# Computing the first batch's attention output already transposed: denominators from products with ones

## The chip, the cores and the metric

The kernel runs on one core of one Trainium2 chip. The metric is device time in microseconds (us), the median of three runs of the whole program. Before the change it is 306.56 us (306.39 to 308.27).

The engines are named as the profile names them: PE is the matrix engine and PEld its weight loads, DVE the vector engine, ACT the scalar engine, POOL the GpSimd engine (here it copies a little and issues most of the transfers that convert float32 to bfloat16), SP the engine that issues the other transfers.

## The reference, cut to what matters

A sparse attention over 8 batches, 8 heads, 576 positions and 64 dimensions per head is followed by a two-layer MLP over all 4608 tokens.

```python
scores = scale * np.matmul(q, k.transpose(0, 1, 3, 2))
rel = pos[:, None] - pos[None, :]
mask_local   = (rel >= 0) & (rel < 32)                         # heads 0 to 3
mask_strided = (rel >= 0) & (pos[None, :] % 32 == pos[:, None] % 32)   # heads 4 to 7
attn = softmax(where(mask, scores, -1e9))
x = (attn @ v).transpose(0, 2, 1, 3).reshape(B * S, H * D)     # 4608 x 512
h = x @ w_in                                                   # 512 -> 2048
out = (h * np.tanh(softplus(h))) @ w_out                       # 2048 -> 512
```

The MLP needs x with its 512 features on the partitions, which the kernel calls xT: four groups of 128 features (cc 0 and 1 from the local heads, cc 2 and 3 from the strided heads) by the tokens.

## The kernel before

The tokens pass through the MLP in nine blocks of 512. While block t passes, the attention of batch t+1 is done in between. Only the attention of batch 0 has nothing to hide behind: until its xT is there, the MLP cannot start. That opening, and block 0 with the attention of batch 1, are what the change touches.

In the opening, the mask is first put into PSUM by a product with the identity ("bias"), the score products are added to it, and ACT takes exp. The probabilities P then serve as the stationary operand, v (with a 65th column of ones, which gives the denominator) as the moving one. So x comes out with the tokens on the partitions, is divided by the denominator, and is transposed on PE afterwards:

```python
def pv_mm(self, kind, i, po):
    for h in range(4):
        ...
        nc.tensor.matmul(po[:, h, :], lhsT=pt[0:n, c0:c0 + 128], rhs=rhs, start=True, stop=True)

def pv2(self, kind, i, i_acc):
    po = acc(i_acc, "po2")[:, :, 0:4 * (D + 1)].rearrange("p e (h d) -> p e h d", h=4)
    ...
    nc.vector.reciprocal(rden[0:m], po[0:m, :, :, D])            # 8 denominators per partition
    nc.vector.tensor_tensor(out=dst..., in0=po[0:m, :, :, 0:D],
        in1=rden[0:m].unsqueeze(3).to_broadcast([m, 2, 4, D]), op=ALU.mult)

def xt(self, kind, hf, eng=None):
    tr = tile_t("trx")[:].bitcast(BF16)
    ...   # 6 or 8 transposes on PE, then one cast into xT
```

The opening itself, from the score products on (cut):

```python
for i in range(3):
    a.qk([("s", i)], i)               # strided scores and exp
copy_v_str01(0, Dv, 0, 4)             # strided v into its layout of 65 columns, on DVE
copy_v_str01(0, Dv, 4, 8)
fill(tile_t("fill"), 2)               # products of zeros
a.pv2("s", 0, 0)
t_step_loc0(kl0, kTl[:, 0, 32:32 + S], 0, Dv)     # local k transposed
t_step_loc0(kl0, kTl[:, 1, 32:32 + S], 1, Sc)
a.pv2("s", 2, 1)
a.pv2("s", 4, 2)
...
t_step_loc0(ql0, qTl[:, 0, :], 0, Sc)             # local q transposed
t_step_loc0(ql0, qTl[:, 1, :], 1, Sc)
a.pv2("s", 6, 0)
a.bias("l", 0, 1)                     # local masks, scores, exp
...
a.xt("s", 0, Dv)
a.xt("s", 1)
Sc.preload_act_table(AF.Mish)
a.pv2("l", 0, 1)
a.pv2("l", 2, 0)
a.pv2("l", 4, 1)
accs = (2, 0, 1)
gT, g1 = mlp1(0, accs)
g1.pop(0)()                           # first hidden group, cc 2 and 3
a.xt("l", 0)
g1.pop(0)()                           # second hidden group, cc 2 and 3
a.xt("l", 1)
```

There are three large PSUM buffers (acc 0 to 2, two banks each) and two small ones (tile_t, one bank each). They hold the scores, the products with v and, later, the MLP's sums in turn. The MLP's second layer of block 0 goes through w_out in quarters: sixteen products with the first quarter, then sixteen with the second, and so on.

Of the kernel before, what the change touches and what calls it, by code (L numbers as in the profile page):

```python
# [10 lines left out]
F32 = mybir.dt.float32  # L11
BF16 = mybir.dt.bfloat16
# [28 lines left out]
def kernel(ctx, tc, q, k, v, moe_w_in, moe_w_out, out):  # L41
# [35 lines left out]
    P_s = [const.tile([PN, 2, n * PN + 56], BF16, name=f"Ps{i}") for i, n in enumerate((7, 7, 4))]  # L77
    P_l = [const.tile([128, 2, n * WQ + 32], BF16, name=f"Pl{i}") for i, n in enumerate((5, 5, 2))]
    x_l = const.tile([128, NW, 256], BF16, name="x_l")
    x_s = const.tile([128, CS, 256], BF16, name="x_s")  # L80
# [53 lines left out]

    def load_v_loc01(b, w0, w1):
        for w in range(w0, w1):
            nc.gpsimd.dma_start(
                vl[b][32:128, w, :, 0:D], v[b, 0:4, WQ * w:WQ * w + WQ].rearrange("h p d -> p h d")
            )

    def load_v_loc_h(b):
# [4 lines left out]

    def rows_v_loc01(b, w0, w1, eng):
        w0, x = max(w0, 1), vl[b % 2]
        cast(eng, x[0:32, w0:w1, :, 0:D], x[96:128, w0 - 1:w1 - 1, :, 0:D])

# [32 lines left out]
    def cast(eng, out_, in_):  # L183
        if eng is nc.scalar:
            nc.scalar.copy(out_, in_)  # L185
        else:
            eng.tensor_copy(out_, in_)  # L187
# [102 lines left out]
    PARTS["n"] = [S_UNITS[0:7], S_UNITS[7:14], S_UNITS[14:16]]  # L290
    AT = {kd: {u: (i, n) for i, p in enumerate(PARTS[kd]) for n, u in enumerate(p)} for kd in "sln"}

    class Attn:
        def __init__(self, b):
            self.b = b
            self.biased = {}

        def bias(self, kind, i, i_acc):
            ps = self.biased[kind, i] = acc(i_acc, "ps")
            w, n, m = (WQ, 128, loc_b) if kind == "l" else (PN, PN, stm_b)  # L300
            nu = len(PARTS[kind][i])
            for e in range(2):
                nc.tensor.matmul(
                    ps[:, e, 0:nu * w], lhsT=ident[0:n, :],
                    rhs=m.unsqueeze(1).to_broadcast([n, nu, w]), start=True, stop=False,
                )

        def qk(self, parts, i_acc):

            biased = parts[0] in self.biased  # L310

            if i_acc is None:
                ps = [tile_t("ps") for _ in range(2)]
            else:
                t = self.biased[parts[0]] if biased else acc(i_acc, "ps")
                ps = [t[:, 0, :], t[:, 1, :]]
            o, todo = 0, []
            for kind, i in parts:
                w = WQ if kind == "l" else PN
                o0 = o  # L320
                for x, y in PARTS[kind][i]:
                    for e in range(2):
                        r = slice(64 * e, 64 * e + 64)
                        if kind == "l":
                            lhsT, rhs = kTl[r, y, WQ * x:WQ * x + 128], qTl[r, y, WQ * x:WQ * x + WQ]
                        else:
                            c0 = SU * (4 * y + x)
                            lhsT = sT(kTs, self.b + (kind == "n"))[r, c0:c0 + 128]
                            rhs = sT(qTs, self.b + (kind == "n"))[r, c0:c0 + PN]
                        nc.tensor.matmul(  # L330
                            ps[e][:, o:o + w], lhsT=lhsT, rhs=rhs, start=not biased,
                            stop=not biased or (x, y) == PARTS[kind][i][-1],
                        )
                    o += w
                todo.append((kind, i, o0, o - o0))
# [37 lines left out]
        def pv(self, kind, i):  # L373
# [8 lines left out]
                in1=rden[0:m, :].unsqueeze(2).to_broadcast([m, 4, D]), op=ALU.mult,  # L382
            )

        def pv2(self, kind, i, i_acc):

            po = acc(i_acc, "po2")[:, :, 0:4 * (D + 1)].rearrange("p e (h d) -> p e h d", h=4)
            m = WQ if kind == "l" else PN
            for e in range(2):
                self.pv_mm(kind, i + e, po[:, e])  # L390
            dst = (x_l if kind == "l" else x_s)[0:m, i:i + 2, :]
            rden = small.tile([128, 2, 4], F32, tag="rden2", name="rden2")
            nc.vector.reciprocal(rden[0:m], po[0:m, :, :, D])
            nc.vector.tensor_tensor(
                out=dst.rearrange("p e (h d) -> p e h d", h=4), in0=po[0:m, :, :, 0:D],
                in1=rden[0:m].unsqueeze(3).to_broadcast([m, 2, 4, D]), op=ALU.mult,
            )
# [48 lines left out]
        def xt_str_copy(self):  # L446
            t0 = (self.b % RING) * S
            for c in range(2):
                nc.scalar.copy(  # L449
                    xT[:, 2 + c, t0:t0 + S].rearrange("p (n j) -> p j n", j=CS), xs_t[:, :, c, 0:PN]  # L450
                )

    def str_steps(b):

        a = Attn(b)
        V = lambda i: (lambda: a.pv("s", i))
        return [
            [], [V(0)], [V(1)], [V(2)], [V(3)], [V(4)], [V(5)], [V(6)], [V(7), a.xt_str],
        ]
# [22 lines left out]
    def attn_steps(b, x, y, z=None):  # L482
# [6 lines left out]
        s0, s1, sl2, l0, l1 = ("s", 0), ("s", 1), (("s", 2), ("l", 2)), ("l", 0), ("l", 1)  # L489
        if x == y:  # L490
            return [
                [], [Q(x, s0)],
                [M(*s0), Q(x, s1)],
                [V("s", 0)],
                [V("s", 1), M(*s1), Q(x, *sl2)],
                [V("s", 2)],
                [V("s", 3), M("s", 2), M("l", 2), Q(x, l0)],
                [V("s", 4)],
                [V("s", 5), M(*l0), Q(x, l1)],
                [V("s", 6), V("l", 5)],  # L500
                [V("s", 7), V("l", 0), M(*l1)],
                [X("s", 0), V("l", 1)],
                [X("s", 1), V("l", 2)],
                [V("l", 3), V("l", 4)],
                [X("l", 0), X("l", 1)], [],
            ]
        r = [
# [16 lines left out]
        if z is not None:  # L524
            r[12].append(Q(x, ("n", 0)))
            r[13].append(Q(z, ("n", 1)))
            r[15] += [Q(x, ("n", 2)), M("n", 0), M("n", 1), M("n", 2)]
        return r


# [91 lines left out]
    with tc.manual_schedule():  # L622
# [14 lines left out]
        Dv.memset(vl[0][0:32, 0], 0.0)  # L637
        load_v_loc01(0, 0, 3)
        load_w_in(0, 256)
        load_v_loc01(0, 3, 6)  # L640
        load_w_in(256, 512)
        load_w_in(512, 1024)
# [17 lines left out]

        a = Attn(0)
        fill_acc(2, 11)
        for hp in range(2):
            t_step(0, "k", hp, Sc if hp else Dv)
        a.bias("s", 0, 0)
        fill_acc(2, 4)
        for hp in range(2):
            t_step(0, "q", hp, Sc if hp else Dv)
        a.bias("s", 1, 1)
        fill_acc(2, 1)  # L670
        a.bias("s", 2, 2)
        for i in range(3):
            a.qk([("s", i)], i)
        copy_v_str01(0, Dv, 0, 4)
        copy_v_str01(0, Dv, 4, 8)
        fill(tile_t("fill"), 2)
        a.pv2("s", 0, 0)
        t_step_loc0(kl0, kTl[:, 0, 32:32 + S], 0, Dv)
        t_step_loc0(kl0, kTl[:, 1, 32:32 + S], 1, Sc)
        a.pv2("s", 2, 1)  # L680
        a.pv2("s", 4, 2)
        fill_acc(0, 1)
        t_step_loc0(ql0, qTl[:, 0, :], 0, Sc)
        t_step_loc0(ql0, qTl[:, 1, :], 1, Sc)
        a.pv2("s", 6, 0)
        a.bias("l", 0, 1)
        a.bias("l", 1, 2)
        a.qk([("l", 0)], 1)
        a.qk([("l", 1)], 2)
        rows_v_loc01(0, 0, 3, Po)  # L690
        load_w_in(1024, 1536)
        load_w_in(1536, 2048)
        rows_v_loc01(0, 3, 6, Po)
        load_qk_str(1)
        load_w_out(0, 1)
        load_v_str01(1)
        load_qk_loc01(1, rows(kl[1]), rows(ql[1]))
        load_w_out(1, 3)
        load_v_loc_h(1)
        load_w_out(3, 4)  # L700
        a.bias("l", 2, 0)
        a.qk([("l", 2)], 0)
        a.xt("s", 0, Dv)
        a.xt("s", 1)
        Sc.preload_act_table(AF.Mish)
        a.pv2("l", 0, 1)
        a.pv2("l", 2, 0)
        a.pv2("l", 4, 1)
        accs = (2, 0, 1)
        gT, g1 = mlp1(0, accs)  # L710
        g1.pop(0)()
        a.xt("l", 0)
        g1.pop(0)()
        a.xt("l", 1)
        Dv.memset(vl32[0:32], 0.0)
        for x in (ks, qs):
            Dv.memset(x[0][64:SU], 0.0)
        load_qk_str(2)
        rows_v_loc01(1, 0, 6, Po)
        for dst, src in ((kl, k), (ql, q)):  # L720
# [8 lines left out]
        def next_loads():  # L729
            load_qk_str(3)  # L730
            copy_v_str01(2, Po, 0, CS)
            rows_v_loc01(2, 0, 6, Po)

        for t in range(NBLK):
# [4 lines left out]
            if t == 0:  # L739
                ts, at = t_steps1(), attn_steps(1, y, y)  # L740
                at[0] += [lambda: Sc.preload_act_table(AF.Exp)]
                at[1] += [lambda: copy_v_str01(1, nc.vector, 0, CS), next_loads]
                at[2] += ts[4:6]
                at[3] += ts[6:8]
                at[9] += [lambda: str_by_dma(2), lambda: loc_by_dma(2)]
# [77 lines left out]
```

## Time and profile before

| What | Value |
|---|---|
| Time, median of 3 | 306.56 us |
| Span of the profiled run | 306.6 us |
| PE busy | 297.2 us (97%) |
| ACT busy | 182.9 us (60%) |
| DVE busy | 156.8 us (51%) |
| POOL busy | 104.0 us (34%) |
| First product of the MLP | 19.42 us |
| The MLP's first layer runs without a gap from | 22.55 us |
| First product of block 1 | 58.03 us |

The page of the profile gives each engine's busy time, then the chain of work that ended last, then the groups of instructions with the mean duration of one. The timeline of a window lists what each engine did and, in brackets, how long it sat idle before and what ended that. [...] For the opening the timeline matters most, as the shares of the whole span are set by the nine blocks behind it.

### The profile page before, as it was taken

To read this page: it belongs to the slowest core of one execution; us is meant where nothing else is said; L and a number is where in the kernel's file an instruction comes from. 1 tells how busy PE (TensorE), PEld (TensorE's weight loads), DVE (VectorE), ACT (ScalarE), POOL (GpSimd) and SP (SyncE) were. 2 spreads that over 40 slices of the span, in tenths; PEclk is the share of its full clock that TensorE was granted. 3 is DMA by queue.
4 is the path that set the end of the run, shared out by engine and by line. 5 is a ranking of instruction groups with operands and counts; after the bars stand their busy time and mean duration, and the time that the engine had idled before them with its cause. 6 is when DMAs were issued, how large, how long until landed. Compare 5 with 4: busy or idle time off the path is not lost.

```text
span 306.6 us, 5875 instructions
## 1 busy us (share of the span) xinstructions
PE 297.2 (97%) x2431; PEld 154.4 (50%) x2431; DVE 156.8 (51%) x375; ACT 182.9 (60%) x196; POOL 104.0 (34%) x120
## 2 busy tenths in 40 slices
PE   8889999999999999999999999999999999999995
PEld 3544555544554445444578654445444544444444
DVE  3572358201850086579877888787879850000000
ACT  5576553767446763767866786687668746216501
POOL 8592326741246025502980297029600000000000
PEclk9999999999999999999999999999999999999999
DMA  7999999999999999999969996997430120011011
GB/s 112 168 145 201 204 168 145 151 119 186 212 210 134 209 147 209 200 197 193 168 152 179 196 170 147 167 193 125 126 90 0 46 92 0 2 68 68 0 71 68
DMA packets 97558, 41.66 MB, mean 136 GB/s; under 512 B 79612, under 2 KB 91612, under 8 KB 97532
## 3 DMA queue, kind: packets, MB, share of 16 engines
q1 hardware_dynamic: 71564, 28.58, 52.6%
q0 software_dynamic: 25680, 12.46, 35.8%
q8 instruction: 19, 0.31, 0.4%
q10 hardware_dynamic: 288, 0.25, 0.3%
q14 instruction: 7, 0.06, 0.1%
HBM read 36.82 MB, written 9.44 MB: 151 GB/s over the span
## 4 chain that ended last, share of the span: by engine, by line
PE 80%; DMA 11%; DVE 4%; POOL 2%; issue 1%; ACT 0%; POOLq 0%
PE psh L562 36%; PE pso L585 33%; DMA w_out<-in_moe_w_out_dram 5%; PE pso L612 5%; PE po L368 4%; DMA w_in<-in_moe_w_in_dram 3%; DMA lq<-in_q_dram 3%; PE ps L330 3%; DVE x_s L380 1%; DVE Pl L352 1%; DVE x_l L380 1%; DVE rden L379 1%; PE trx L407 1%; POOL w_in L172 0%; POOL ks L110 0%
## 5 line engine op out<-in xcount | busy, mean ns | idle before, releaser
L562 PE MATMUL psh<-xT,w_in 128*128 128x512 bf16 (+1 forms) x640 | 130.6, 358 | 1.0 <-ACT xT L185 0.7
L585 PE MATMUL pso<-w_out,gT 128*128 128x512 bf16 x512 | 121.7, 379 | 0.2 <-DMA w_out<-in_moe_w_out_dram 0.2
L568 ACT ACTIVATE gT<-psh 128x1024 bf16<-128x1024 f32 x72 | 72.4, 1023 | 47.7 <-PE psh L562 47.7
L562 PEld LDWEIGHTS <-w_in 128*128 128x128 bf16 x640 | 60.1, 98 | 56.6 <-issue 1.4
L585 PEld LDWEIGHTS <-gT 128*128 128x128 bf16 x512 | 45.5, 98 | 46.2 <-issue 0.2
L442 DVE STREAM_TRANSPOSE xs_t<-x_s 32x512 bf16<-32x512 bf16 x48 | 33.7, 702 | 0.9
L592 ACT COPY osb<-pso 128x1024 f32<-128x1024 f32 x16 | 17.6, 1099 | 24.6 <-PE pso L585 14.0
L379 DVE RECIPROCAL rden<-po 72x4 f32<-72x4 f32 (+1 forms) x98 | 17.3, 177 | 28.2 <-PE po L368 27.9
L187 POOL CAST kl<-kl 96x768 bf16<-96x768 f32 x10 | 8.5, 876 | 62.3 <-DMA kl<-in_k_dram 53.0
L352 DVE TENSOR_TENSOR Ps<-Ps,consts_sb 72x864 bf16<-72x864 bf16 (+3 forms) x12 | 8.1, 683 | 38.9 <-ACT Ps L344 38.9
L433 DVE STREAM_TRANSPOSE xT<-x_l 32x384 bf16<-32x384 bf16 x48 | 27.3, 569 | 0.7
L187 DVE COPY osb<-pso 128x512 f32<-128x512 f32 (+1 forms) x2 | 1.1, 558 | 51.3 <-PE pso L612 51.3
L380 DVE TENSOR_TENSOR x_s<-po,rden 72x256 bf16<-72x256 f32 x56 | 23.6, 421 | 1.9
L344 ACT ACTIVATE Ps<-ps 72x864 bf16<-72x864 f32 (+3 forms) x21 | 17.4, 860 | 10.7 <-PE ps L330 10.6
L449 ACT COPY xT<-xs_t 128x576 bf16<-128x576 bf16 x8 | 21.4, 2938 | 0.0
L368 PEld LDWEIGHTS <-Ps 72*128 72x128 bf16 x256 | 14.9, 98 | 11.5 <-DVE Ps L352 0.8
L344 ACT ACTIVATE Pl<-ps 128x960 bf16<-128x960 f32 (+1 forms) x20 | 17.1, 875 | 3.7 <-PE ps L330 3.6
L380 DVE TENSOR_TENSOR x_l<-po,rden 96x256 bf16<-96x256 f32 x42 | 17.7, 421 | 1.4
L185 ACT COPY xT<-trx 128x576 bf16<-128x576 bf16 x15 | 9.5, 640 | 14.3 <-PE trx L417 11.7
L368 PE MATMUL po<-vs,Ps 72*128 72x65 bf16 x256 | 17.3, 194 | 0.1
L187 POOL CAST vl<-vl 128x768 bf16<-128x768 f32 (+2 forms) x20 | 15.4, 770 | 4.9 <-DMA vl<-in_v_dram 4.0
L352 POOL TENSOR_TENSOR Ps<-Ps,consts_sb 72x1008 bf16<-72x1008 bf16 (+1 forms) x9 | 14.5, 1650 | 0.1
(90 smaller groups left out, 236.0 us busy)
## 6 DMA issues: line engine op xcount, KB each, us to landing
out_dram<-osb SPq DMA_DIRECT2D x16, 512.0 KB, 4.2
kl<-in_k_dram SPq DMA_DIRECT2D x5, 576.0 KB, 6.9
ql<-in_q_dram SPq DMA_DIRECT2D x5, 576.0 KB, 9.9
vs<-in_v_dram SPq DMA_DIRECT2D x5, 576.0 KB
vl<-in_v_dram SPq DMA_DIRECT2D x5, 576.0 KB, 9.7
w_out<-in_moe_w_out_dram POOLq DMA_DIRECT2D x4, 512.0 KB, 15.9
ks<-in_k_dram POOLq DMA_DIRECT2D x7, 288.0 KB, 9.5
qs<-in_q_dram POOLq DMA_DIRECT2D x7, 288.0 KB, 9.3
```

Of the source, the lines that this page charges most:

```text
L187: eng.tensor_copy(out_, in_)
L344: nc.scalar.activation(pt[0:n, :, 0:nw], t[0:n, :, o0:o0 + nw], AF.Exp, scale=scale)
L352: meng.tensor_tensor(out=pm, in0=pm, in1=mk[0:n, :].unsqueeze(1).unsqueeze(1).to_broadcast([n, 2, nu, w]), op=ALU.mult,)
L368: nc.tensor.matmul(po[:, h, :], lhsT=pt[0:n, c0:c0 + 128], rhs=rhs, start=True, stop=True,)
L379: nc.vector.reciprocal(rden[0:m, :], po[0:m, :, D])
L380: nc.vector.tensor_tensor(out=dst.rearrange("p (h d) -> p h d", h=4), in0=po[0:m, :, 0:D], in1=rden[0:m, :].unsqueeze(2).to_broadcast([m, ...
L433: nc.vector.transpose(dst[32 * q:32 * q + 32, :, :, m:m + 32], src[m:m + 32, :, :, q, :])
L442: nc.vector.transpose(xs_t[32 * q:32 * q + 32, :, :, m:m + 32], src[m:m + 32, :, :, q, :])
L449: nc.scalar.copy(xT[:, 2 + c, t0:t0 + S].rearrange("p (n j) -> p j n", j=CS), xs_t[:, :, c, 0:PN])
L562: nc.tensor.matmul(ps[:, u, o:o + n], lhsT=w_in[:, cc, fc * 128:(fc + 1) * 128], rhs=xT[:, cc, a:a + n], start=(cc == 2 and o == 0), stop= ...
L568: nc.scalar.activation(gT[:, 2 * g:2 * g + 2, :], ps[:], AF.Mish)
L585: nc.tensor.matmul(p[:, ot % 2, :], lhsT=gT[:, fc, 128 * ot:128 * ot + 128], rhs=w_out[:, fc, :], start=(fc == 0), stop=(fc == 15),)
```

## The change

Batch 0's attention is written anew (class First). v becomes the stationary operand and the probabilities the moving one, so the product has v's 64 dimensions on the partitions and the tokens along the row: x comes out as xT, and the transposes of x and their casts are not needed. The denominators can then no longer come from a 65th column. They come from products of a matrix of ones (64 columns) with the same probabilities, which puts each token's denominator on all 64 partitions of its head. DVE takes the reciprocals of that whole tile and multiplies.

Beside it: strided v is used as it was loaded, without a copy; the local v of batch 0 is loaded by heads in four transfers where there were six; w_in's first two pieces become one; in block 0 the transposes of batch 1's local q and k move to later steps (attn_steps1), and w_out's second quarter is issued ahead of that q and k.

The diff, cut to its core:

```diff
+    ones = const.tile([128, 2, D], BF16, name="ones")
...
-    def rows_v_loc01(b, w0, w1, eng):
-        w0, x = max(w0, 1), vl[b % 2]
-        cast(eng, x[0:32, w0:w1, :, 0:D], x[96:128, w0 - 1:w1 - 1, :, 0:D])
+    def rows_v_loc01(b, hp, eng):
+        x = vl[b % 2][:, :, 2 * hp:2 * hp + 2, 0:D]
+        cast(eng, x[0:32, 1:NW], x[96:128, 0:NW - 1])
...
+    Z_UNITS = [(jj, h) for h in range(4) for jj in range(4)]
+    Y_UNITS = [(i, hp) for hp in range(2) for i in range(NW)]
+    PARTS["z"] = [Z_UNITS[0:6], Z_UNITS[6:12], Z_UNITS[12:16]]
+    PARTS["y"] = [Y_UNITS[2:7], Y_UNITS[7:12], Y_UNITS[0:2]]
...
+    class First:
...   (open, scores, exp: the mask, the score products and exp as before)
+        def z_num(self, c, num, parts):
...
+                        nc.tensor.matmul(
+                            num[64 * (h % 2):64 * (h % 2) + 64, e, PN * jj:PN * jj + PN],
+                            lhsT=vsd[0][:, v0:v0 + 64],
+                            rhs=P_s[part][0:PN, e, PN * u:PN * u + PN], start=True, stop=True,
+                        )
+        def z_den(self, c, den):
...
+                        nc.tensor.matmul(
+                            den[64 * (h % 2):64 * (h % 2) + 64, e, PN * js[0]:PN * (js[-1] + 1)],
+                            lhsT=ones[0:PN, 0, :],
+                            rhs=P_s[part][0:PN, e, PN * u0:PN * (u0 + len(js))],
+                            start=True, stop=True,
+                        )
+        def z_inv(self, den, rd):
+            nc.vector.reciprocal(
+                rd[:, 0:576].rearrange("p (e n) -> p e n", e=2), den[:, :, 0:4 * PN]
+            )
+        def z_mul(self, c, num, rd):
+            nc.vector.tensor_tensor(
+                out=xT[:, 2 + c, 0:S].rearrange("p (n j e) -> p e j n", j=4, e=2),
+                in0=num[:, :, 0:4 * PN].rearrange("p e (j n) -> p e j n", j=4),
+                in1=rd[:, 0:576].rearrange("p (e j n) -> p e j n", e=2, j=4), op=ALU.mult,
+            )
+        def y_pv(self, i, num, den):
...   (products with ones and with v for one part of the local heads)
+        def y_norm(self, i, num, den, rd):
+            units = PARTS["y"][i]
+            nc.vector.reciprocal(rd[:, 0:WQ * len(units)], den[:, 0:WQ * len(units)])
+            for hp in range(2):
...
+                    nc.vector.tensor_tensor(
+                        out=xT[:, hp, w0:w0 + b - a], in0=num[:, a:b], in1=rd[:, a:b], op=ALU.mult
+                    )
...
+    def attn_steps1(y, ts, vs_copy, loads):
...
+            [V("s", 2), ts[0], ts[1]],
+            [V("s", 3), M("s", 2), ts[2], ts[3]],
...
-        load_v_loc01(0, 0, 3)
-        load_w_in(0, 256)
-        load_v_loc01(0, 3, 6)
-        load_w_in(256, 512)
+        load_v_loc_h(0)
+        load_w_in(0, 512)
         load_w_in(512, 1024)
...   (the opening)
+            a.scores("z", i)
+            a.exp("z", i)
         fill(tile_t("fill"), 2)
+        n2 = acc(0, "num")
+        a.z_num(0, n2, (0,))
+        d2 = acc(1, "den")
+        a.z_den(0, d2)
+        a.z_inv(d2, rd[0])
+        a.z_num(0, n2, (1,))
+        a.z_mul(0, n2, rd[0])
+        t_step_loc0(kl0, kTl[:, 0, 32:32 + S], 0, Sc)
+        n3 = acc(2, "num")
+        a.z_num(1, n3, (1, 2))
         t_step_loc0(kl0, kTl[:, 1, 32:32 + S], 1, Sc)
+        d3 = acc(1, "den")
+        a.z_den(1, d3)
+        a.z_inv(d3, rd[1])
+        rows_v_loc01(0, 0, Po)
+        rows_v_loc01(0, 1, Po)
         load_w_in(1024, 1536)
         load_w_in(1536, 2048)
-        rows_v_loc01(0, 3, 6, Po)
         load_qk_str(1)
         load_w_out(0, 1)
         load_v_str01(1)
+        load_w_out(1, 2)
         load_qk_loc01(1, rows(kl[1]), rows(ql[1]))
-        load_w_out(1, 3)
+        load_w_out(2, 3)
         load_v_loc_h(1)
         load_w_out(3, 4)
+        t_step_loc0(ql0, qTl[:, 0, :], 0, Sc)
+        t_step_loc0(ql0, qTl[:, 1, :], 1, Dv)
+        a.z_mul(1, n3, rd[1])
+        for i, n in ((2, 0), (0, 1), (1, 2)):
+            a.open("y", i, acc(n, "ps"))
+            a.scores("y", i)
+            a.exp("y", i)
         Sc.preload_act_table(AF.Mish)
+        ty = tile_t("po")
+        a.y_pv(2, ty[:, 2 * WQ:4 * WQ], ty[:, 0:2 * WQ])
+        a.y_norm(2, ty[:, 2 * WQ:4 * WQ], ty[:, 0:2 * WQ], rd[0][:, 576:])
+        for i in range(2):
+            ty = acc(i + 1, "po")
+            a.y_pv(i, ty[:, 1, :], ty[:, 0, :])
+            a.y_norm(i, ty[:, 1, :], ty[:, 0, :], rd[i])
+        accs = (0, 1, 2)
         gT, g1 = mlp1(0, accs)
         g1.pop(0)()
-        a.xt("l", 0)
         g1.pop(0)()
-        a.xt("l", 1)
```

## The prediction

> **What bounds the kernel now.** I read the page's first part (busy shares), then the chain of work that ended last, then the timeline of the first 60 us. PE is busy 97% of the span, and from 58 us on the chain is products of the MLP's two layers and nothing else. So whatever this change does is done before block 1's first product (58.03 us in the timeline), and it reaches the end as it stands there.
>
> ```profile
> PE 297.2 (97%) x2431; PEld 154.4 (50%) x2431; DVE 156.8 (51%) x375; ACT 182.9 (60%) x196; POOL 104.0 (34%) x120
> PE 80%; DMA 11%; DVE 4%; POOL 2%; issue 1%; ACT 0%; POOLq 0%
> ```
>
> The timeline of the opening (start, duration, engine, line, operation; in brackets the idle time before it and what ended that) shows where the MLP starts.
>
> ```profile
> 17.04 0.69 PE L417 MATMUL trx<-consts_sb,x_s 72*128 72x72 bf16 x16
> 19.42 1.02 PE L562 MATMUL psh<-xT,w_in 128*128 128x512 bf16 x4
> 20.28 0.42 PE L407 MATMUL trx<-consts_sb,x_l 96*128 96x96 bf16 x6
> 20.54 1.03 PE L562 MATMUL psh<-xT,w_in 128*128 128x512 bf16 x4
> 21.41 0.42 PE L407 MATMUL trx<-consts_sb,x_l 96*128 96x96 bf16 x6
> 22.55 9.66 PE L562 MATMUL psh<-xT,w_in 128*128 128x512 bf16 x44 [0.73 <-ACT xT L185]
> ```
>
> Eight products of the first hidden groups (cc 2 and 3) come early. The other 56 can run once the local x is in xT, at 22.55 us. One of them takes 9.66 / 44 = 0.22 us. So the number to predict is the moment at which **the last piece of local x is written**. Later, three transfers hold PE up: strided q of batch 1, its local q, and w_out's second quarter.
>
> ```profile
> 33.60 0.43 PE L243 MATMUL tr<-consts_sb,qs 72*128 72x72 bf16 x8 [0.27 <-DMA qs<-in_q_dram]
> 40.19 0.31 PEld L259 LDWEIGHTS <-ql 96*64 96x64 bf16 x12 [0.22 <-DMA ql<-in_q_dram]
> 43.12 1.02 PE L585 MATMUL pso<-w_out,gT 128*128 128x512 bf16 x4 [0.22 <-DMA w_out<-in_moe_w_out_dram]
> ```
>
> **The new cost: reciprocals of whole tiles.** The groups of instructions by shape give DVE's costs (mean ns before the second bar).
>
> ```profile
> L379 DVE RECIPROCAL rden<-po 72x4 f32<-72x4 f32 x56 | 9.9, 178 | 16.9 <-PE po L368 16.8
> L393 DVE RECIPROCAL rden<-po 72x8 f32<-72x8 f32 x4 | 0.8, 196 | 1.1 <-PE po L368 1.1
> L187 DVE COPY osb<-pso 128x256 f32<-128x256 f32 x1 | 0.4, 424 | 4.5 <-PE pso L612 4.5
> L187 DVE COPY osb<-pso 128x512 f32<-128x512 f32 x1 | 0.7, 692 | 46.8 <-PE pso L612 46.8
> L380 DVE TENSOR_TENSOR x_s<-po,rden 72x256 bf16<-72x256 f32 x56 | 23.6, 421 | 1.9
> L394 DVE TENSOR_TENSOR x_s<-po,rden 72x512 bf16<-72x512 f32 x4 | 2.7, 686 | 0.1
> ```
>
> A copy out of PSUM costs (692 - 424) / 256 = 1.05 ns per element and 424 - 268 = 156 ns fixed; a multiplication costs 1.04 ns and the same 156. A reciprocal of 8 elements is 18 ns dearer than one of 4, which is 4.5 ns per element. With the fixed 156 ns of the other two, it is (196 - 156) / 8 = 5.0. The two ways agree, and I take **4.9 ns per element**: five times a copy. In the kernel before nobody sees this, since a reciprocal there has 4 or 8 elements. After the change it has 192 to 576.
>
> [...] the first eleven filling products took 4.88 / 11 = 0.44 us each, four later ones 1.03 / 4 = 0.26.
>
> ```profile
> 1.26 4.88 PE L534 MATMUL fill<-kTs 128*128 128x512 bf16 x11 [1.26 <-DVE kTs L634]
> 6.90 1.03 PE L534 MATMUL fill<-kTs 128*128 128x512 bf16 x4
> ```
>
> **The change part by part.**
>
> Removed: 56 products of 65 columns and 28 transposes of x on PE (16 of the first kind take 0.66 us, 16 strided transposes 0.69, so some 3.6 us in all), four casts into xT, two copies of strided v (1.02), seven reciprocals (1.4) and seven multiplications (4.8) on DVE.
>
> Added on PE: 32 + 24 products with 64 columns of v held still, about 1.8 us at the rate of the products removed, and products with ones over 2 x 1152 columns (strided) and 2 x 1152 (local): 4608 columns at 0.22 us per 512, or 2.0 us. PE's sum hardly changes.
>
> Added on DVE: reciprocals of 576 (twice), 192 and 480 (twice). At 156 ns + 4.9 ns they are 2.98, 2.98, 1.10, 2.51 and 2.51, in all **12.1 us**. Multiplications of 576 (twice), 192, 384 + 96 and 480: 0.76, 0.76, 0.36, 0.82, 0.66.
>
> On the path. The second exp of the strided scores ends at 12.2 us (2.20 us for three, from 10.50). The six products with ones take 0.5 us and 0.2 to land. From 12.95 us DVE is the chain:
>
> - first reciprocal to 15.93, multiplication to 16.69, second reciprocal to 19.67 (its denominators wait for the buffer that the first one reads, but are there by 16.6)
> - copy of local q, 0.76 like the k copy of that shape, to 20.43; multiplication to 21.2
> - this frees the third large buffer. PE puts mask and scores of the last local part there and does the small part's products: about 1.2 us, DVE idle, to 22.4
> - small part: 1.10 + 0.36, to 23.9; part 0: 2.51 + 0.82, to 27.2; part 1: 2.51 + 0.66, to 30.4
>
> The 56 products then start at about **30.5 us instead of 22.55: 8.0 us later**. The first hidden group's early products (24 us) don't help, and the second's must wait until 27.2 for the buffer that part 0 leaves.
>
> Given back. By then the transfers have long landed, so the three waits above (0.27 + 0.22 + 0.22) go. The move of batch 1's local transposes away from the first steps of block 0 takes out some more small stalls: from 36.12 to 43.12 us PE did 16 products (3.5 us) and about 2 us of attention in 7.0 us, so 1.5 us were lost, 0.44 of it in the two waits named. Part comes back as the transposes contend for the two small buffers later. I give this stage 1.2 us in all, with the first wait. w_out's second quarter sooner is worth nothing beyond its 0.22 when the MLP itself starts so late. Sum: +8.0 - 1.2 = **+6.8 us**.
>
> Clock: between about 24 and 30.5 us PE has 0.9 us of work, and it may fall to half rate. [...] At a chance of one in three this adds 0.5 us. 306.6 + 6.8 + 0.5 = **313.8 us**.
>
> **The rivals.**
>
> 1. *A reciprocal is flat*: the 18 ns between 4 and 8 elements come from the access pattern's extra dimension, and long ones run at 1.05 ns. Then the five take 0.76, 0.76, 0.36, 0.66, 0.66 = 3.2 us. The same walk ends with PE's products one after another: the last probabilities at about 19.1, products of part 1 to 20.2, then all 64 of the MLP's first layer from 20.15 without a gap, which equals 56 from 21.9. That is 0.7 us sooner, with the 1.2 us of the later stage about 304.7. For it: the order of the new opening looks laid out for this. Against it: the multiplication over two banks (512 elements) shows no cost for its extra dimensions.
>
> 2. *The transfers pace block 0 anyway*: strided q of batch 1 landed at 33.6 us, exactly when PE wanted it, so an earlier MLP would only wait there. This caps a gain under rival 1 at some 1 to 2 us, or near zero (306) if q doesn't land sooner. Fewer and larger early transfers and a POOL less held up speak for sooner. It makes no difference if DVE delays the start by 8 us.
>
> 3. *DVE overlaps more than I allow*: part of the reciprocals lies beside exp and PE work. In my walk only 1.2 us of DVE idleness is left after 12.95 us, so hiding has no room.
>
> **Range and chances.** I give the dear reciprocal 0.87. Within it, slopes of 4.5 to 5.5 ns move the sum by -1.0 to +1.4 us, the stage's recovery by +-0.7[...]: about 311 to 316.5 us. The limit of 2% is 312.7 us, so about four fifths of that case is over it: slower 0.70. The rest of it and rival 1 with rival 2 (304.5 to 306.5) are within 2%: 0.29. Faster by over 2% would need 300.4 us, a gain of 6 us, which no part of the change has to give: 0.01.
>
> **What would show it.** The reciprocals' rows in the changed kernel: 128x576 near 3.0 us and 128x480 near 2.5 bear me out; 0.76 and 0.66 make rival 1 right. The long row of first-layer products should start at 30.5 us with DVE's xT named as what ended the wait. Block 1 should start near 64.8 us. PE's share before 30 us should be low, and if the clock fell, the first ones of those products take 0.44 us each. I'd be wrong if a long reciprocal is cheap, or if the recovery in block 0 is several us.

## The result, and the profile after

The changed kernel takes **327.02 us**, the median of four runs (326.35 to 327.62). The kernel before took 306.50 beside it (306.39 to 308.27). The ratio is **1.0655, interval 1.0608 to 1.0701**: 6.6% slower. (Here and below a ratio comes from the undisturbed executions of both kernels side by side, so it isn't quite the quotient of the two medians.) The prediction had the direction, but its range ended at 316.5 us.

The first and second parts of the page of the changed kernel, and the chain's shares by engine:

```profile
PE 302.2 (93%) x2422; PEld 155.9 (48%) x2422; DVE 170.2 (52%) x371; ACT 181.8 (56%) x194; POOL 101.6 (31%) x119
PE   7546599799999999999999999999999999999996
PEclk9855699999999999999999999999999999999999
PE 84%; DVE 11%; DMA 2%; ACT 1%; issue 1%; POOL 1%; DVEq 0%; ACTq 0%; POOLq 0%
```

A digit of the slices stands for 8.1 us here. PE is poorly used in the first five and nearly full afterwards, so most of the loss lies in the first 41 us. There the granted clock falls to half as well. DVE's share of the chain has gone from 4% to 11%.

The chain of waits of the changed kernel (start, duration, engine, what it works on, line) says who holds that time:

```profile
12.57 3.77 DVE x_s L487
...
16.43 2.72 DVE xT L492
19.15 3.33 DVE x_l L487
...
23.10 2.62 DVE xT L492
...
29.49 3.08 DVE x_s L523
...
33.31 3.08 DVE x_l L523
...
37.12 12.51 PE psh L651 x47
```

L487 and L523 are reciprocals, L492 the multiplications of the strided heads that write xT. (Where two pieces overlap, the chain counts from the end of the first.) Of the 24.55 us from 12.57 to 37.12 the chain gives DVE 22.3: one lane, in which each item waits for the one before it. PE's part, between the second L492 and the first L523, is 2.0 us. The long row of first-layer products, which began at 22.55 us before, begins at 37.12.

Three moments cut each trace into stages; the same ones serve for every kernel below.

| Kernel | Long row starts | Second layer starts | Block 1 starts | Span |
|---|---|---|---|---|
| before | 22.55 | 36.12 | 58.03 | 306.6 |
| after | 37.12 | 52.24 | 76.51 | 324.6 |
| difference of the stage | +14.57 | +1.55 | +2.36 | |

The sum at block 1 is +18.5 us. The medians differ by 20.5, mostly because the execution of before that was profiled happened to take 308.33 us, 1.8 over its median; time minus span is 1.7 us in both profiled executions.

### The profile page after: what moved, and what is told of

Read it like the earlier page. It is cut to its first block, busy times and chain, and to the rows that moved or that the text cites. A ratio compares the mean times of both kernels' runs of the same rounds, so it can differ in the third digit from the quotient of the medians.

```text
span 324.6 us, 5853 instructions
## 1 busy us (share of the span) xinstructions
PE 302.2 (93%) x2422; PEld 155.9 (48%) x2422; DVE 170.2 (52%) x371; ACT 181.8 (56%) x194; POOL 101.6 (31%) x119
## 4 chain that ended last, share of the span: by engine, by line
PE 84%; DVE 11%; DMA 2%; ACT 1%; issue 1%; POOL 1%; DVEq 0%; ACTq 0%; POOLq 0%
PE psh L651 38%; PE pso L674 32%; PE pso L701 4%; PE po L353 4%; PE ps L316 3%; DVE xT L492 2%; DMA qs<-in_q_dram 2%; DVE x_s L523 1%; DVE x_s L487 1%; DVE x_l L365 1%; DVE x_l L487 1%; DVE x_l L523 1%; DVE x_s L365 1%; DVE rden L364 1%; DVE xT L528 1%
## 5 line engine op out<-in xcount | busy, mean ns | idle before, releaser
L651 PE MATMUL psh<-xT,w_in 128*128 128x512 bf16 (+1 forms) x640 | 133.7, 363 | 5.0 <-DVE xT L528 4.7
L681 ACT COPY osb<-pso 128x1024 f32<-128x1024 f32 x16 | 17.6, 1097 | 24.7 <-PE pso L674 14.2
L329 ACT ACTIVATE Ps<-ps 72x1008 bf16<-72x1008 f32 (+3 forms) x18 | 15.2, 871 | 10.4 <-PE ps L316 10.3
L353 PEld LDWEIGHTS <-Ps 72*128 72x128 bf16 x224 | 13.7, 98 | 11.9 <-issue 1.2
L182 POOL CAST vl<-vl 128x768 bf16<-128x768 f32 (+2 forms) x20 | 16.5, 824 | 5.6 <-DMA vl<-in_v_dram 4.6
L353 PE MATMUL po<-vs,Ps 72*128 72x65 bf16 x224 | 15.9, 194 | 0.9 <-DVE kTl L182 0.9
L329 ACT ACTIVATE Pl<-ps 128x960 bf16<-128x960 f32 (+1 forms) x16 | 14.4, 913 | 2.9 <-PE ps L316 2.9
L180 ACT COPY xT<-trx 128x576 bf16<-128x576 bf16 x12 | 7.7, 639 | 12.2 <-PE trx L388 9.9
## 6 DMA issues: line engine op xcount, KB each, us to landing
w_out<-in_moe_w_out_dram POOLq DMA_DIRECT2D x4, 512.0 KB, 13.5
```

The lines of the kernel that those rows point to most:

```text
L329: nc.scalar.activation(pt[0:n, :, 0:nw], t[0:n, :, o0:o0 + nw], AF.Exp, scale=scale)
L651: nc.tensor.matmul(ps[:, u, o:o + n], lhsT=w_in[:, cc, fc * 128:(fc + 1) * 128], rhs=xT[:, cc, a:a + n], start=(cc == 2 and o == 0), stop= ...
```

## The experiments

The predicted mechanism, a reciprocal of whole tiles on DVE as the new chain, was visible at once. Open was why the loss was nearly three times the predicted one. The theories: **R**, the reciprocal costs more per element than I took; **W**, the multiplication that writes xT is slowed by the order in which it writes; **C**, PE's clock falls as PE has too little to do; **B**, block 0 itself got slower, by its new order of steps or by a collision of DVE with POOL.

### The order of the write alone

Tokens n and j of the strided heads are apart in the product but interleaved in xT. The change walks the tile in the product's order, so each 2-byte result lands 16 bytes past the last. Here it is walked in xT's order: strided reads, a write in sequence.

```diff
-    out=xT[:, 2 + c, 0:S].rearrange("p (n j e) -> p e j n", j=4, e=2),
-    in0=num[...].rearrange("p e (j n) -> p e j n", j=4),
+    out=xT[:, 2 + c, 0:S].rearrange("p (n j e) -> p n j e", j=4, e=2),
+    in0=num[...].rearrange("p e (j n) -> p n j e", j=4),      # in1 likewise
```

> Edit: the two multiplications of the strided heads run in the order of the output, so that bf16 is written without a stride and the two inputs are read with one; nothing else. Theory 1 (the strided 2-byte write costs 4.7 ns per element, as a copy with such a write did on ACT before: 2.94 us): the two fall from 2.70 us to some 0.76 us each, the long row of first-layer products starts near 33.2 us instead of 37.1, and the time falls by about 4 us to 323. Theory 2 (it is the four-dimensional pattern, or two float32 inputs, whatever the order): they stay at 2.7 us or get slower, and the time stays at 327.

It took 322.45 us, ratio to before 1.0491 (1.0422 to 1.0561); that is 4.6 us less than the changed kernel. Groups by shape on DVE (busy us, mean ns), first from the changed kernel, then from this one; the second of each pair is within 50 ns of it:

```profile
L492 DVE TENSOR_TENSOR xT<-num,x_s 128x576 bf16<-128x576 f32 x1 | 2.7, 2718 | 0.1
```

```profile
L492 DVE TENSOR_TENSOR xT<-num,x_s 128x576 bf16<-128x576 f32 x1 | 1.2, 1171 | 0.1
```

The same 576 products take 1.15 instead of 2.70 us. W holds: two of them give 3.1 us, and the long row starts 2.9 sooner, at 34.20. Another 1.0 us is gained in block 0 (23.27 instead of 24.27 us); the run of POOL's copy, below, shows what that is.

### No reordering at all

To part the cost of a strided read from that of the plain operation, xT is written as the product lies. This leaves out the interleaving of the tokens.

```diff
-    out=xT[:, 2 + c, 0:S].rearrange("p (n j e) -> p e j n", j=4, e=2),
+    out=xT[:, 2 + c, 0:S].rearrange("p (e j n) -> p e j n", j=4, e=2),
```

> Edit: the changed kernel, whose two multiplications of the strided heads read as before but write one element behind the other, so the tokens of these heads stay in the order of the score tiles (the reordering is left out). Theory 1 (only the write with a step of 16 bytes is slow): both take 0.76 us, against 2.70 with the strided write and 1.15 with strided reads, and the time is 322 to 323. Theory 2 (two float32 inputs of 576 over two banks are slow by themselves): they stay over 1.5 us.

```profile
L492 DVE TENSOR_TENSOR xT<-num,x_s 128x576 bf16<-128x576 f32 x1 | 0.8, 757 | 0.1
```

That is the group of this kernel (the second one took 741 ns): 0.75 us, the prediction's 0.76. So the write in steps of 16 bytes costs 1.95 us per 576 elements, 3.4 ns each; the strided reads of the experiment before cost 0.4. No other step was tried, so why such a write is slow, and from which step on, isn't shown. The whole kernel took 322.47 us (ratio 1.0517, 1.0486 to 1.0547), the same as the one before: its long row starts 1.07 us sooner and its block 1 0.72 us sooner, which the medians don't show.

### Copies in place of the reciprocals

The five reciprocals become copies of the same shapes. This leaves out the division by the softmax's sums; everything else stays.

```diff
-    nc.vector.reciprocal(rd..., den...)
+    nc.vector.tensor_copy(rd..., den...)
```

> Edit: each of the five long reciprocals becomes a copy of the same tile to the same place, so the division is left out (x is multiplied by the denominators); the strided multiplications stay slow. Theory 1 (the reciprocals' 15.1 us lie one behind the other on the path): copies take 0.76, 0.76, 0.36, 0.66 and 0.66 us, 3.2 in all, the MLP's row starts about 12 us sooner, near 25 us, PE's clock falls less, and the time is 313 to 315 us. Theory 2 (something else holds the opening, such as exp or w_in's landing): the row starts later than 27 us and the time stays above 317.

It took 312.60 us, ratio 1.0171 (1.0103 to 1.0238), 14.4 us less than the changed kernel. Groups by shape of the changed kernel, and then of this one:

```profile
L487 DVE RECIPROCAL x_s<-den 128x576 f32<-128x576 f32 x1 | 3.8, 3758 | 3.3 <-PE den L479 3.3
L523 DVE RECIPROCAL x_s<-po 128x192 f32<-128x192 f32 x1 | 1.4, 1357 | 2.0 <-PE po L515 2.0
```

```profile
L487 DVE COPY x_s<-den 128x576 f32<-128x576 f32 x1 | 0.8, 758 | 3.3 <-PE den L479 3.3
```

Between 192 and 576 elements the reciprocal grows by (3758 - 1357) / 384 = **6.25 ns per element** over 157 ns fixed, and the ones of 480 elements lie on that line (3157 worked out, 3146 and 3148 measured). The second one of 576 took 3683 here, but 3747 and 3756 in the two runs above. R holds: 6.25, not 4.9. The long row, which now has all 64 products in it, starts at 23.47 us.

### Both together

> Edit: the two edits before together (division left out, output written in order). This is the world that the prediction called rival 1. Theory 1 (DVE's two slow operations and the clock that falls while PE waits for them are all of the opening's loss): the 64 first-layer products run from about 20.2 to 21 us without a gap, at full clock, and the time is 304.5 to 307. Theory 2 (block 0 with its new order has lost time of its own, whatever the opening does): the opening is as early, but block 0 takes some 24 us instead of 22 and the time is 307 to 309.

With copies and the write in order (the division is left out again) it took 307.54 us, ratio 1.0014 (0.9993 to 1.0035). The two savings alone were 14.4 and 4.6 us, 19.0 in all; together they are 19.5. That they add up so well is in part luck. Each run alone had already lost the collision in block 0 (23.42 and 23.27 us instead of 24.27), which can be saved only once; and only with both does the granted clock stay at 1.00 (with copies alone it is 0.71 from 15 to 20 us and 0.61 from 20 to 25). From the timeline of this kernel:

```profile
19.42 12.41 PE L651 MATMUL psh<-xT,w_in 128*128 128x512 bf16 x56
34.44 1.89 PE L674 MATMUL pso<-w_out,gT 128*128 128x512 bf16 x8
```

The row starts at 19.42 without a gap, 0.7 sooner than the prediction's rival of a cheap reciprocal had it. It has all 64 products in it, so, at 0.22 us for each of the other eight, it is worth 56 from 21.15. Yet block 1 starts at 57.61 us. Even with the division at the cost of a copy the change gains nothing: something takes it back in block 0.

### The rest without the turn

The kernel before, with all of the change except the transposed product: the new loads, the new order of block 0, w_out's second quarter sooner.

```diff
 (kernel before)
+    load_v_loc_h(0); load_w_in(0, 512)         # v by heads, w_in in one piece
+    load_w_out(1, 2)                           # ahead of batch 1's local q and k
+    at = attn_steps1(y, ts[4:8], ..., next_loads)
```

> Edit: the kernel before with all of the change but the turned products: local v by heads, w_in's first two pieces as one, w_out's second quarter ahead, batch 1's local transposes at later steps. Theory 1 (the prediction's share for this stage): the waits for batch 1's strided q, local q and w_out's second quarter shrink and the time falls by 0.5 to 1.2 us, to 305.4 to 306. Theory 2 (the later transposes and POOL's copies collide with DVE's masks in block 0 as they do in the changed kernel): block 0 takes 24 us and the time rises to 308 or 309.

It took 308.49 us, ratio 1.0041 (1.0023 to 1.0060): the rest alone makes the kernel slower by 0.4%. Block 0 (second layer to block 1) took 23.17 us, the same as with both (23.17), against 21.91 before.

### The loads alone

```diff
 (kernel before)
+    load_v_loc_h(0); load_w_in(0, 512)
```

> Edit: the kernel before with only the loads of the opening changed: local v by heads in four transfers, w_in's first two pieces as one, the copies of v's rows by pairs of heads. Block 0 keeps its old order, and w_out's second quarter its old place. Theory 1 (in the run with the rest of the change the MLP's second layer began 0.84 us sooner, and block 0's new order gave 1.3 us back): the time falls by 0.5 to 0.9 us, to 0.997 to 0.9985 of before. Theory 2 (w_out's second quarter or local q lands no sooner than before, so PE waits where it waited): no change, 0.999 to 1.001.

306.68 us, ratio 0.9991 (0.9978 to 1.0005): nothing that can be measured. In its trace PE doesn't wait for strided q, local q or w_out at all, and block 0 takes 21.35 us. Whether the loads or the particular execution removed those waits stays open. The medians are the same, and the profiled execution of before was 1.8 us over its median, so the waits may be peculiar to that execution.

### Both, with the old order of block 0

```diff
 (both together)
-    at = attn_steps1(y, ts[4:8], ..., next_loads)
+    at = attn_steps(1, y, y); at[2] += ts[4:6]; at[3] += ts[6:8]     # as before; w_out too
```

> Edit: the kernel without division and with the output written in order, but with block 0 and the order of w_out's transfers as before the change. The division is still left out. Theory 1 (the new order of block 0 loses 1.2 us, as steps with two transposes wait for the two small buffers while DVE is at x): block 0 takes some 22 us instead of 23.1, and the time is 305 to 306, about 1.2 us under the run with the new order. Theory 2 (block 0 is paced by transfers, so the order does not matter): it stays at 307 to 307.5.

305.97 us, ratio 0.9953 (0.9935 to 0.9971), still without the division. Block 0 takes 21.36 us. The chain of waits shows why. With the new order (both together):

```profile
41.87 0.43 DVE x_s L365
...
42.43 0.45 PE tr L254 x12
...
44.22 0.43 DVE x_s L365
...
44.70 0.45 PE tr L254 x12
...
47.90 0.43 DVE x_s L365
...
48.37 0.26 PE ps L316 x3
```

With the old order (this kernel):

```profile
39.99 0.43 DVE x_s L365
...
40.47 0.45 PE tr L254 x12
```

There are two small PSUM buffers. A product with v (po) takes one until DVE has divided it out. A step that has such a product and two transposes (tr) needs three turns, so PE stands still for DVE's 0.19 + 0.43 us. The old order has one such step; the new one has two, and puts the last local scores (ps, from 48.37) into the small buffers besides. Over block 0 DVE holds 3.00 us of the chain with the new order and 1.75 with the old one; the handing over between engines holds 0.57 and 0.29, PE's own work 18.85 and 18.54. The order of w_out's transfers differs too, but in neither trace does PE wait for a transfer in block 0. Block 0 is 1.8 us longer in the trace, and the kernel 1.6 us in the medians.

### PE kept busy in the opening

The changed kernel with 56 more products of zeros into spare turns of a small buffer, for C.

```diff
+    fill(tile_t("fill"), 11)                  # before the second denominators
+    fill(tile_t("fill"), (10, 7, 5)[i])       # before each of the local masks
+    fill(tile_t("fill"), 13)                  # between the early first-layer groups
+    fill(tile_t("fill"), 10)                  # ahead of the long row
```

> Edit: the changed kernel with 56 filling products of zeros (11, 5, 10, 7, 13 and 10) in the gaps in which PE waits for DVE in the opening; nothing else. Theory 1 (PE's clock falls to half in those gaps, and the MLP's first row of products starts on it): the row runs at 0.22 us per product from its first one, 2.4 us sooner through, and the time falls from 327 to about 324.6. Theory 2 (the row's first products are slow because w_in or xT is read by others at the time): they stay at 0.43 us and the time stays at 327.

322.41 us, ratio 1.0515 (1.0484 to 1.0545), 4.6 us less than the changed kernel. The windows of the changed kernel (window, length, busy time of PE, PEld, DVE, ACT and POOL with counts, granted clock, DMA's share, GB/s):

```profile
15.00:20.00 5.00, 2.41 (x34) 1.89 (x34) 4.89 (x3) 0.64 (x1) 4.00 (x6) 0.50 1.19 179
20.00:25.00 5.00, 1.47 (x12) 0.58 (x12) 5.00 (x3) 1.44 (x2) 3.97 (x6) 0.50 1.23 200
```

PE is busy 2.41 and 1.47 us in 5, and its clock is granted at 0.50. It is 0.50 in the next window too, 0.84 from 30 to 35 us and 0.50 again from 35 to 40, where the long row begins. Some windows of 1 us, and the timeline in front of the row:

```profile
14.00:15.00 1.00, 0.00 (x0) 0.00 (x0) 1.00 (x1) 0.17 (x1) 0.00 (x0) 0.66 1.51 151
31.00:32.00 1.00, 0.13 (x1) 0.00 (x0) 1.00 (x1) 0.00 (x0) 0.72 (x1) 0.81 1.26 195
34.00:35.00 1.00, 0.62 (x3) 0.20 (x2) 1.00 (x1) 0.00 (x0) 0.71 (x1) 0.90 1.26 203
35.00:36.00 1.00, 0.00 (x0) 0.00 (x0) 1.00 (x1) 0.00 (x0) 0.02 (x1) 0.50 1.29 202
41.00:42.00 1.00, 1.00 (x5) 0.39 (x4) 0.00 (x0) 0.33 (x1) 0.67 (x2) 0.69 3.07 136
```

```profile
33.37 1.25 PE L651 MATMUL psh<-xT,w_in 128*128 128x512 bf16 x5 [2.24 <-DVE xT L528]
37.12 12.51 PE L651 MATMUL psh<-xT,w_in 128*128 128x512 bf16 x47 [2.50 <-DVE xT L528]
```

In windows of 0.2 us around these moments the clock is 1.00 or 0.50 but for the one in which it changes (0.80 from 14.2 to 14.4 us, 0.53 from 31.2 to 31.4, 0.94 from 41.6 to 41.8). So it fell twice. At 14.3 us it fell, 0.8 us into a pause of 2.9 us (13.5 to 16.4) in which PE waited for the first reciprocal. It was back at 31.4 us, and at 34.8 it fell again, 0.2 us into the pause of 2.5 us in front of the row. The row pays for this second fall: it runs at half clock from 37.1 to 41.6 us.

With the filling products, its slices of the page and its timeline:

```profile
PEclk9999999999999999999999999999999999999999
```

```profile
36.68 10.30 PE L651 MATMUL psh<-xT,w_in 128*128 128x512 bf16 x47 [0.34 <-DVE xT L528]
49.59 1.90 PE L674 MATMUL pso<-w_out,gT 128*128 128x512 bf16 x8
```

From the long row to the second layer it now takes 12.91 instead of 15.12 us: **the fallen clock cost 2.2 us there**, and 0.44 in the opening. That is 2.65 of the 3.6 us by which the spans differ (324.6 and 321.0). The further 1.1 went in block 0 (23.17 instead of 24.27), which is the collision of the next experiment, missed here because everything came sooner. C holds, but it follows from DVE's lane and isn't an independent cause: with both savings on DVE the clock stays at 1.00 without filling products.

### POOL's copy moved later

In block 0 of the changed kernel a mask multiplication of DVE takes 1.77 us, elsewhere 0.44. POOL copies strided v at that time. The copy was to be put at the end of block 0:

```diff
-    copy_v_str01(2, Po, 0, CS)               # in step 1's loads
+    at[15] += [lambda: copy_v_str01(2, Po, 0, CS)]
```

> Edit: the changed kernel, with POOL's copies of batch 2's v moved from the second step of block 0 to its end. Theory 1 (DVE's mask of 1.77 us in block 0, 0.45 before the change, waits [...]): the mask takes some 0.45 us again, block 0 shortens by 1.1 us, and the time falls from 327 to 325.5 to 326.2. Theory 2 (the mask is slow for another reason, such as the clock or transfers): it still takes 1.7 us and the time stays at 327.

The edit didn't do this: in both traces what ends POOL's wait ahead of the copy (2.55 and 4.39 us) is its transfer, not one of PE's steps. Here that was 1.6 us later, which need not be the edit's doing, since in the other runs of the turned kernel with the new order of block 0 it lies anywhere from 60.8 to 64.0 us. Still, the copy no longer lies beside the mask. From the timeline of the changed kernel and then of this one:

```profile
61.94 1.89 POOL L182 COPY vs<-vs 72x2048 bf16<-72x2048 bf16 x1 [2.55 <-DMA vs<-in_v_dram]
62.36 1.77 DVE L337 TENSOR_TENSOR Ps<-Ps,consts_sb 72x576 bf16<-72x576 bf16 x1
64.86 0.28 PE L353 MATMUL po<-vs,Ps 72*128 72x65 bf16 x4 [0.94 <-DVE kTl L182]
```

```profile
62.80 0.44 DVE L337 TENSOR_TENSOR Ps<-Ps,consts_sb 72x576 bf16<-72x576 bf16 x1
...
63.51 1.89 POOL L182 COPY vs<-vs 72x2048 bf16<-72x2048 bf16 x1 [4.39 <-DMA vs<-in_v_dram]
```

With the copy behind it the mask takes 0.44 us and block 0 23.18 instead of 24.27. The other five runs of the turned kernel with the new order of block 0 have no copy beside this mask either, and it takes 0.44 or 0.45 us in each. In the changed kernel the mask, begun 0.42 us into the copy, ends at 64.13, 0.30 us after the copy; PE waits 0.94 us for DVE. So it took 1.77 us beside the copy and 0.44 without it; why isn't shown. The time was 326.21 us (ratio 1.0610, 1.0552 to 1.0667), which isn't told apart from the changed kernel's; which run meets the collision is a matter of when a transfer lands.

### The division moved to ACT

The runs so far pointed to a version that keeps the turned product and takes the reciprocals off DVE: 1/x as exp(-ln x) on ACT, which was busy for 5.4 of the 25 us from 15 to 40 us in the changed kernel. Four of the five are done so; the small part's, of 192 elements, stays on DVE. The write is in order, block 0 and w_out as before, local k's copies go to DVE, and the MLP's table is loaded after the opening. This computes all of the reference.

```diff
-    nc.vector.reciprocal(r, den)
+    nc.scalar.activation(r, den, AF.Ln)
+    nc.scalar.activation(r, r, AF.Exp, scale=-1.0)
-    Sc.preload_act_table(AF.Exp)
+    Sc.preload_act_table_set("natural_log_exp_and_others")   # one set with both
```

> Edit: the whole computation, turned as in the change, but four of the five long reciprocals are taken on ACT as exp(-ln(x)) (one table set with both functions), the output is written in order, local k is copied by DVE, and block 0 has its old order. Theory 1 (the turn fails only for DVE's slow operations): two passes of some 0.65 us on ACT take the place of 3.7 us, local x is ready near 22 to 23.5 us, and the time is 305.5 to 307.5. Theory 2 (ACT, which also takes six exps and a copy in the opening, becomes the bound): local x is ready after 25 us and the time is over 309.

306.50 us against 306.96 for the kernel before beside it, ratio **0.9971 (0.9954 to 0.9989)**: faster than both kernels, though against the one before by 0.3% only. Its timeline:

```profile
12.57 0.65 ACT L488 ACTIVATE x_s<-den 128x576 f32<-128x576 f32 x1
...
13.26 0.68 ACT L489 ACTIVATE x_s<-x_s 128x576 f32<-128x576 f32 x1
...
21.16 4.06 PE L673 MATMUL psh<-xT,w_in 128*128 128x512 bf16 x18 [0.28 <-DVE xT L533]
```

Two passes on ACT, 1.33 us, do what took DVE 3.76. ACT's groups of the first 30 us have two table loads of 1283 ns, this set's and the MLP's: the logarithms and exps of the opening ran on the one load. The long row starts at 21.16 us instead of 37.12. That this is still worth only 0.3% is what the run with the old order of block 0 had shown: even with copies in place of the division the turned product came to 0.9953.

## Why the prediction was wrong

The moments of all kernels (us from the span's start):

| Kernel | Long row starts | Second layer | Block 1 | Median |
|---|---|---|---|---|
| after | 37.12 | 52.24 | 76.51 | 327.02 |
| POOL's copy later | 36.92 | 52.67 | 75.85 | 326.21 |
| PE kept busy | 36.68 | 49.59 | 72.76 | 322.41 |
| write in order | 34.20 | 49.36 | 72.63 | 322.45 |
| no reordering | 33.13 | 48.74 | 71.91 | 322.47 |
| copies for reciprocals | 23.47 | 38.55 | 61.97 | 312.60 |
| both together | 19.42 | 34.44 | 57.61 | 307.54 |
| both, old block 0 | 19.38 | 34.41 | 55.77 | 305.97 |
| division on ACT | 21.16 | 35.16 | 56.45 | 306.50 |
| the rest without the turn | 22.16 | 35.28 | 58.45 | 308.49 |
| the loads alone | 22.22 | 35.35 | 56.70 | 306.68 |

With copies for the reciprocals the long row has all 64 products in it, with the division on ACT 60, elsewhere 55 or 56, so the first column compares like with like only among the last.

Laid out as a ladder of medians: before 306.96 (in the other sets of runs 306.50 to 306.90), with the turned product, the new loads, copies for the division and a write in order 305.97, with the new order of block 0 307.54, with the division 322.45, with the changed order of the write 327.02. The steps are **-1.0, +1.6, +14.9 and +4.6 us**. The step of the division includes the fallen clock, and the last one the collision of DVE with POOL, 1.0.

**Right.** DVE was the chain; the reciprocal was dear (the rival of a flat reciprocal falls with the 1357, 3146 and 3758 ns); DVE's xT ended the wait before the long row; transfers played no part (one weight load, at 60.20 us, is put down to local q, but its step takes 2.51 us, as in the run of both together, which has no such wait); PE doesn't wait for w_out's second quarter, in its old place or its new one, in any run after the change. The order of the walk held, and it began at 12.57 us instead of 12.95. Of its gaps, PE's turn in front of the small part took 2.0 us instead of 1.2, at half clock; with the filling products it took 1.3.

**Wrong, by its own terms.** Four steps failed. Together they make the range too low.

*First, "I take 4.9 ns per element".* It is 6.25, and the five took 15.09 us instead of 12.1: **+3.0**. The step was an extrapolation from 4 and 8 elements to 576. On the line that the long ones give, the short ones would take 182 and 207 ns; they took 178 and 196. So differences of 4 and 11 ns there became 3 us here. The second way, which seemed to confirm the first, used the same 196 ns. The range allowed 5.5 ns at most.

*Second, the multiplications of 576 at "0.76, 0.76".* They took 2.72 and 2.68: **+3.9**. The cost was taken from a multiplication whose write is contiguous, and the access pattern wasn't looked at. The groups of the kernel before had the same pattern on another engine, in the ACT copy that interleaves later batches' tokens into xT; below it the other copy of that size:

```profile
L449 ACT COPY xT<-xs_t 128x576 bf16<-128x576 bf16 x8 | 21.4, 2938 | 0.0
L185 ACT COPY xT<-trx 128x576 bf16<-128x576 bf16 x15 | 9.5, 640 | 14.3 <-PE trx L417 11.7
```

2938 against 640 ns for as many elements was the warning. (The two differ in their source too, SBUF and PSUM; that the order of the write is what costs was shown on DVE alone.)

*Third, "I give this stage 1.2 us in all"* as recovery, counted over the row and block 0. The row without the fallen clock took 12.91 us (filling products) against 13.57 before, so 0.66 was less there. But 0.22 of it is one product more that ran ahead of the row, and the other 0.44 is missing in the loads' run as well (13.13 us for the same 56 products as before), whose median is that of before. And block 0 took 2.36 more: 1.26 for the new order (1.8 against the runs in which PE doesn't wait for transfers), 1.1 for the collision. Transposes and products with v take the same two buffers; the prediction had that as a deduction from the recovery, and it was larger than the recovery. The collision wasn't foreseen. The waits that were to go are absent in the loads' run too, without a gain: probably they, and most of the recovery worked out from that trace, were peculiar to an execution 1.8 us over its median. -1.2 became +1.7: **+2.9**.

*Fourth, "At a chance of one in three this adds 0.5 us".* Chance and size were the author's estimate and rest on no trace: in the one of before the granted clock is 1.00 throughout the opening. The clock did fall, and it cost more. It fell 0.8 and 0.2 us into pauses of 2.9 and 2.5 us, so the pauses that DVE's lane leaves were enough, and the row ran at half clock for 4.5 us. It cost 2.2 in the row and 0.44 before it: **+2.1**. (Of the clock at the program's start only the durations speak, 0.44 us per filling product; the record of the granted clock has 1.00 there.)

The four and the earlier start are 3.0 + 3.9 + 2.9 + 2.1 - 0.4 = 11.5 us. The traces differ by 18.5 at block 1, where 7.3 was predicted: 11.2. The medians are 327.0 - 313.8 = 13.2 apart from the prediction; most of the remaining 2.0 is the 1.8 by which the profiled execution of before, from which the prediction was worked out, was over its median.

## What to carry to other kernels

Before an operation goes on the path, look for its shape and its access pattern in the profile, on any engine: a strided write, and a slope drawn from two small sizes, each cost this estimate 3 to 4 us. When one engine becomes the lane, what it delays may not be all it costs: here PE's clock fell too (2.65 us), and a mask of DVE met a copy of POOL (1.1 us). And when a change has several parts, run the part that is said to help by itself: here the turned product, with the division at the cost of a copy, gained 1 us, and the reordering around it took 1.6. Waits seen in one execution are worth recovering only if that execution is a typical one.

## What the runs showed of the hardware

- A DVE reciprocal of float32 out of PSUM: 157 ns + 6.25 ns per element from 192 to 576 elements, six times a copy's slope (in whole, 3758 against 758 ns for 576 elements). On ACT logarithm and exp of the same tile take 0.65 + 0.68 us.
- A 2-byte write at steps of 16 bytes: 2.70 us instead of 0.75 for 576 elements on DVE. A copy on ACT with such a write took 2.94, another one of that size, from PSUM and in order, 0.64. Reading at large steps and writing in sequence on DVE: 1.15.
- PE's granted clock fell from 1.00 to 0.50 within 0.8 and 0.2 us of the start of pauses of 2.9 and 2.5 us. With PE busy for 2.41 and 1.47 us of the next two stretches of 5 us it stayed at 0.50; in the long row it came back after 4.5 us.
- A mask multiplication of DVE with two operands in SBUF took 1.77 us instead of 0.44 beside a copy by POOL.
